# Attention scores by halves of the queries: four quarter tiles of 196 columns, four heads at a time

## The chip, the cores and the metric

The kernel runs on one core of a Trainium2 chip. The metric is the time of one execution on the device in microseconds (us); lower is better. The core has a matrix engine (TensorE: PE for the matmuls, PEld for the weight loads that go with them), a vector engine (DVE), an activation engine (ACT), GpSimd (POOL) and a queue processor (SP) that issues most of the DMAs. Matmuls write to PSUM, which has eight banks of 512 float32 per partition.

## The reference, cut to what matters

```python
scores = scale * np.matmul(q, k.transpose(0, 1, 3, 2))     # batch 2, heads 8, sequence 768, head size 64
is_sink = pos[None, :] < int(n_sink)                       # n_sink 4
in_window = (rel >= 0) & (rel < int(window))               # rel = query - key, window 128
scores = np.where(is_sink | in_window, scores, -1000000000.0)
a = np.exp(scores - np.max(scores, axis=-1, keepdims=True))
a = a / (np.sum(a, axis=-1, keepdims=True) + 1e-09)
x = np.matmul(a, v)
...
x = _moe_ref(x=x, ...)       # 1536 tokens routed to 8 experts of fixed capacity, two layers each
return _moe2_ref(x=x, ...)   # a feed-forward layer with SiLU, 512 to 2048 to 512
```

Each query sees the four sink keys and the 128 keys that end at itself. A block of 128 queries therefore needs its own 128 keys and the 128 of the block before, and of each key place only one of the two: the key of the block before where it lies behind the query's place, the own one otherwise.

## The kernel before

The attention is the first stage. It runs over 12 blocks of 128 queries (2 batches of NB = 6), and in a block over H = 8 heads; a head with its block is a step, n = 0 to 95 (i = n // 8 is the block, j = i % 6 its place in the batch, h = n % 8 the head). The code is one loop over n that writes out the instructions of all engines, and every engine works through its own in the order in which they were written:

- `s_mm` writes the scores by matmuls in float32 (line L261), two heads at a time: it is called at even n. A head has 64 rows of q and k, so two heads lie side by side on the 128 rows of the array (`o` = 0, 1). For j > 0 a matmul makes 264 columns: four sinks and 128 keys of the block before, then the same of the own block. Each head has a bank, a tile of the pool `s`, which holds four tiles and turns in a ring.
- `s_merge` (L267, DVE) overwrites, in the own block's scores, those of the keys that lie behind the query (`later`) by those of the block before. For j = 0 there is nothing to merge.
- `s_max` (L274, DVE) adds the mask, scales and takes the maximum; `s_exp` (L283, ACT) takes the exponential two steps on.
- `tr` (L297, PE) transposes the weights five steps on, and `tr_out` copies them out (ACT) and cuts them into two triangles (POOL); `pv` (L343, L345, L348, PE) multiplies them with the values 13 steps on; `finish` scales on DVE (L370, L366, L377).
- Every eight steps a few more matmuls write to tiles of the pool `s`: `sink_tr` (L326), `vw` (L385, four column quarters of the array with 32 columns each) and `vw_tr` (L396).
- DVE also unpacks weights that come as 64-bit floats (L915 to L931). These instructions are bound to steps: the first one stands at n = 27.
- SP issues the loads (kall, qr, vt, va of a block, then raw weights) in the written order. Eight semaphores serve them in turn, so that a load waits until the one eight before it has landed.

After the attention come the routing (it begins in its last steps), a gather by DMA, the experts and the last feed-forward layer.

Of the kernel before, what the change touches and what calls it, by code (L numbers as in the profile page):

```python
# [11 lines left out]
F32 = mybir.dt.float32  # L12
F32R = mybir.dt.float32r
BF = mybir.dt.bfloat16
I32 = mybir.dt.int32
AF = mybir.ActivationFunctionType
OP = mybir.AluOpType
# [4 lines left out]
P = 128  # L22
B, H, S, D = 2, 8, 768, 64
# [3 lines left out]
KW = P + 4  # L27
# [152 lines left out]


VW = D + E + 1
HH = H // 2
LT, LP, LS = 5, 13, 6
LATE = 9, 10
# [4 lines left out]
PB = {"s": 4, "tp": 2, "X": 2}  # L190
# [3 lines left out]
def attention_band(tc, qd, kd, va_d, vt_d, vs_d, sel_d, wbd_d, eye_d, n_sink, ident, x_d, L_sb, pp, hooks={}):  # L194
    nc = tc.nc
    with ExitStack() as ctx:
        cp = ctx.enter_context(tc.tile_pool(name="a_c", bufs=1))
        wp = ctx.enter_context(tc.tile_pool(name="a_w", bufs=2))

        kall = cp.tile([P, NB, HH, KW], F32, name="kall")  # L200
        va = cp.tile([P, NB, H, VW], F32, name="va")
        vts, Q = {}, {}

        def load(i, step=HH):
            b, j = divmod(i, NB)
# [18 lines left out]
        nc.scalar.dma_start(eye, eye_d)  # L224
        vsf = [cp.tile([97, H, VW], F32, name=f"vsf{b}") for b in range(B)]
        for b in range(B):
# [5 lines left out]
        load(2)  # L232
        vsr = [cp.tile([97, H, VW], F32R, name=f"vsr{b}") for b in range(B)]

        later = cp.tile([P, P], F32, name="later")
        nc.gpsimd.memset(later, 1.0)
        nc.gpsimd.affine_select(out=later, in_=later, pattern=[[1, P]], compare_op=OP.is_gt, fill=0.0, base=0,
                                channel_multiplier=-1)
        mask = cp.tile([P, 3, KW], F32, name="mask")
        nc.gpsimd.memset(mask, 0.0)  # L240
        if n_sink < 4:
            nc.gpsimd.memset(mask[:, :, n_sink:4], NEG)
        nc.gpsimd.affine_select(out=mask[:, 0, 4:], in_=mask[:, 0, 4:], pattern=[[-1, P]], compare_op=OP.is_ge,
                                fill=NEG, base=0, channel_multiplier=1)
        nc.gpsimd.memset(mask[:, 0, 4:4 + n_sink], NEG)
        nc.gpsimd.affine_select(out=mask[:, 1, 4:4 + n_sink], in_=mask[:, 1, 4:4 + n_sink], pattern=[[-1, n_sink]],
                                compare_op=OP.is_ge, fill=NEG, base=0, channel_multiplier=1)

        A, TS, AT, X, XS, LW, VT = {}, {}, {}, {}, {}, {}, {}
        ats = [cp.tile([97, P], F32R, name=f"ats{k}") for k in range(2)]  # L250
        for t in ats:
            nc.gpsimd.tensor_copy(t[96:97, :], later[0:1, 0:1].to_broadcast([1, P]))

        def s_mm(n):
            i, h = divmod(n, H)
            j = i % NB
            b0 = max(j - 1, 0)
            for o in range(2):
                s = pp.tile([P, 512], F32, name="s", bufs=PB["s"])[:, :2 * KW].rearrange("p (a k) -> p a k", a=2)
                d = slice(o * D, (o + 1) * D)  # L260
                nc.tensor.matmul(s[:, :j - b0 + 1], Q[i][d, h // 2], kall[d, b0:j + 1, h // 2], start=True, stop=True)  # L261
                TS[n + o] = s

        def s_merge(n):
            s = TS[n]
            if n // H % NB:
                nc.vector.copy_predicated(s[:, 1, 4:], later.bitcast(I32), s[:, 0, 4:])  # L267

        def s_max(n):
            j = n // H % NB  # L270
            s = TS[n]
            t = wp.tile([P, KW], F32, name="t", bufs=4)
            nm = wp.tile([P, 1], F32, name="nm", bufs=6)
            nc.vector.tensor_tensor_reduce(t, s[:, 1 if j else 0], mask[:, min(j, 2)], -1.0 / math.sqrt(D), 3.0e38,  # L274
                                           OP.add, OP.min, nm)
            TS[n] = t, nm

# [54 lines left out]
        def pv(n):  # L332
# [3 lines left out]
            if r == 0:  # L336
                if (i, g) == (NT - 1, 0):
                    X[i, g] = misc(HH * VW).rearrange("p (h v) -> p h v", h=HH)
                else:
# [82 lines left out]
        NH = NT * H  # L422
        for n in range(NH + LP + 5):
            i, h = divmod(n, H)
            if n < NH and n % 2 == 0:
                s_mm(n)
            if n < len(WARM) - 1:
                warm(WARM[n + 1])
            for f in hooks.get(n, ()):
                if f is None:  # L430
                    while dve_now:
                        feed(dve_now)
                else:
                    f()
            if 0 <= n - 2 < NH:
                s_exp(n - 2)
            if 0 <= n - LT < NH:
                tr(n - LT)
            feed(act_now, act_bg)
            if n < NH and n % 2 == 0:  # L440
                s_merge(n)
                s_merge(n + 1)
            feed(dve_now, dve_bg)
            if n < NH:
                s_max(n)
            feed(dve_now, dve_bg)
            feed(act_now, act_bg)
            for _ in range(3 if n >= NH + LT and n - NH not in LATE else 0):
                feed(act_late)
            it, ht = divmod(n - LS, H)  # L450
            if ht == H - 1 and 0 <= it < NT:
                sink_tr(it)
            if n < NH and h == 0:
                if i == 1:
                    nc.sync.dma_start(vsf[1][:96], vs_d[:96, 1])
                if i + 2 < NT:
                    load_v(i + 2)
                if i + 3 < NT:
                    load(i + 3)
            for at, f in VWS.get(n, ()):  # L460
                (vw, vw_tr, sinks)[f](*at)
            if 0 <= n - LP < NH:
                pv(n - LP)
# [1219 lines left out]
```

## Time and profile before

| | |
|---|---|
| time, median of 3 runs | 556.95 us (555.79 to 557.17) |
| the profiled execution | 556.44 us, its span 554.7 us |
| granted TensorE clock, mean over the span | 0.996 |
| busy over the span | PE 539.3, PEld 478.5, DVE 352.9, ACT 293.6, POOL 227.5 us |

The span goes from the first to the last instruction; what lies around it is 1.7 us here. Matmuls are pipelined and the records overlap, so a busy PE is not one at its peak. The steps of the attention lie between 4 and 97 us, the rest of it and the routing up to 136 us, and the experts and the last layer behind.

### The profile page before, as it was taken

How to read it: one execution, taken by the hardware profiler on the slowest of the kernel's cores; microseconds unless marked ns; L12 is line 12 of the kernel's file. 1: busy time of each engine (PE TensorE's matmuls, PEld its weight loads, DVE VectorE, ACT ScalarE, POOL GpSimd, SP SyncE). 2: the span in 40 equal slices, each digit the busy share in tenths (PEclk: the TensorE clock that was granted, in tenths of full speed). 3: DMA queues.
4: the chain of work that ended last, by engine and by line, in shares of the span. 5: the costliest groups of instructions: out<-in, count | busy, mean ns of one | idle time of the engine just before them, and what ended most of it. 6: DMA issues, size and time to landing. Idle time of an engine off the chain costs nothing.

```text
span 554.7 us, 9683 instructions
## 1 busy us (share of the span) xinstructions
PE 539.3 (97%) x3389; PEld 478.5 (86%) x3389; DVE 352.9 (64%) x983; ACT 293.6 (53%) x576; POOL 227.5 (41%) x218
## 2 busy tenths in 40 slices
PE   8999999878999999999999999999999999999995
PEld 3778777766999999999999989989888988898884
DVE  3788998874433443443337898876979777863523
ACT  4545454675566876776655364453444444443330
POOL 4434234286699999999994000000000000000404
PEclk9999999999999999999999999999999999999999
DMA  7998762244557667667660464653677856266502
GB/s 206 367 389 267 256 205 81 76 142 150 167 199 234 214 222 230 216 221 229 218 223 3 155 219 119 253 186 97 196 253 247 284 162 239 77 210 231 206 19 113
DMA packets 43935, 107.91 MB, mean 195 GB/s; under 512 B 4650, under 2 KB 12458, under 8 KB 43884
## 3 DMA queue, kind: packets, MB, share of 16 engines
q1 hardware_dynamic: 41696, 100.88, 54.0%
q0 software_dynamic: 1920, 6.29, 3.2%
q8 instruction: 27, 0.44, 0.3%
q14 instruction: 24, 0.20, 0.1%
q10 hardware_dynamic: 268, 0.10, 0.1%
HBM read 86.81 MB, written 20.45 MB: 193 GB/s over the span
## 4 chain that ended last, share of the span: by engine, by line
PE 68%; issue 4%; POOL 2%; DMA 1%; ACT 0%; DVE 0%; POOLq 0%; another core or an unknown queue 0%; DVEq 0%; ACTq 0%
PE h L1276 21%; PE acc L1398 20%; PE mm L1182 9%; PE m L1205 8%; PE mm L1185 4%; PE m L1208 4%; POOL out L1369 2%; PE mm L1205 1%; PE mm L1141 1%; DMA row<-x_d,idx 1%; PE mm L1208 1%; PE m L1182 0%; POOLq L1679 0%; PE m L1141 0%; ACT wr L958 0%
## 5 line engine op out<-in xcount | busy, mean ns | idle before, releaser
L961 POOL TENSOR_TENSOR wr<-raw,wr 128x1024 fp32r<-128x1024 f32 x64 | 150.8, 2387 | 8.0 <-ACT wr L958 7.8
L1398 PE MATMUL acc<-wr,gt 128*128 128x512 f32 x576 | 145.4, 395 | 0.0
L1398 PEld LDWEIGHTS acc<-wr,gt 128*128 128x128 f32 x576 | 107.3, 188 | 19.4
L1369 POOL DMA_INDIRECT out<-raw,idx x12 | 11.6, 968 | 241.3 <-DVE raw L1410 241.1
L1276 PE MATMUL h<-x,wr 128*128 128x384 f32 x528 | 101.3, 338 | 0.0
L1276 PEld LDWEIGHTS h<-x,wr 128*128 128x128 f32 x528 | 93.7, 188 | 4.0 <-DVE keep L1310 0.3
L1182 PE MATMUL mm<-xg,wr 128*128 128x384 f32 x248 | 72.4, 360 | 0.5 <-DVE xg L1156 0.3
L958 ACT ACTIVATE wr<-raw 128x1024 fp32r<-128x1024 f32 x64 | 66.6, 1052 | 1.1 <-ACTq L725 0.9
L1205 PE MATMUL m<-ht,wr 128*128 128x384 f32 x224 | 66.0, 361 | 0.0
L1185 PE MATMUL mm<-xg,wr 128*128 128x192 f32 x248 | 62.2, 251 | 0.0
L1208 PE MATMUL m<-ht,wr 128*128 128x192 f32 x224 | 56.2, 251 | 0.0
L1457 DVE TENSOR_TENSOR gt<-keep,gt 128x384 fp32r<-128x384 f32 x64 | 39.1, 613 | 26.7 <-ACT gt L1263 26.6
L283 ACT ACTIVATE A<-t,nm 128x132 f32<-128x132 f32 x96 | 36.1, 400 | 30.3 <-DVE nm L274 30.2
L1182 PEld LDWEIGHTS mm<-xg,wr 128*128 128x128 f32 x248 | 46.5, 187 | 1.2 <-DVE xg L1156 0.7
L1163 DVE TENSOR_TENSOR mm<-mm,t 128x384 f32<-128x384 f32 x33 | 18.7, 567 | 45.2 <-ACT t L1162 41.7
L1185 PEld LDWEIGHTS mm<-xg,wr 128*128 128x128 f32 x248 | 47.3, 191 | 0.0
L1262 ACT ACTIVATE keep<-keep 128x384 f32<-128x384 f32 x30 | 15.8, 526 | 54.0 <-DVE keep L1310 53.9
L1208 PEld LDWEIGHTS m<-ht,wr 128*128 128x128 f32 x224 | 42.7, 191 | 0.0
L1205 PEld LDWEIGHTS m<-ht,wr 128*128 128x128 f32 x224 | 42.0, 188 | 0.0
L305 POOL TENSOR_SCALAR_AFFINE_SELECT atd<-at 128x512 f32<-128x512 f32 x24 | 16.5, 688 | 58.4 <-ACT at L303 47.1
L1276 PE MATMUL h<-xn,wr 128*128 128x384 f32 x180 | 36.8, 339 | 0.0
L1276 PEld LDWEIGHTS h<-xn,wr 128*128 128x128 f32 x180 | 32.6, 188 | 2.6
(197 smaller groups left out, 939.5 us busy)
## 6 DMA issues: line engine op xcount, KB each, us to landing
raw<-in_w SPq DMA_DIRECT2D x64, 512.0 KB, 3.7
sums_d<-os SPq DMA_DIRECT2D x36, 256.0 KB, 2.0
xn<-mix_d SPq DMA_DIRECT2D x12, 768.0 KB, 5.5
raw<-in_wi SPq DMA_DIRECT2D x16, 512.0 KB, 5.7
raw<-in_wo SPq DMA_DIRECT2D x16, 512.0 KB, 6.2
os<-sums_d SPq DMA_DIRECT2D x24, 256.0 KB, 2.6
mix_d<-xn SPq DMA_DIRECT2D x6, 768.0 KB, 4.3
va<-in_va SPq DMA_DIRECT2D x12, 292.0 KB, 4.4
```

The lines of the kernel that those rows point to most:

```text
L283: nc.scalar.activation(A[i][:, h], t, AF.Exp, bias=nm, scale=-1.0)
L958: nc.scalar.activation(w[:, 0, sl], src(), AF.Copy)
L961: (nc.vector if k in self.late else nc.gpsimd).tensor_tensor(w[:, 1, sl], src(), w[:, 0, sl].bitcast(F32), OP.subtract)
L1163: nc.vector.tensor_tensor(h, h, t, OP.add)
L1182: nc.tensor.matmul(mm[:, b, :2 * CAP], w[:, 0, fb, d, o:o + P], x[:, d].rearrange("p a t -> p (a t)"), start=d == 0, stop=False, skip_grou ...
L1185: nc.tensor.matmul(mm[:, b, :CAP], w[:, 1, fb, d, o:o + P], x[:, d, 0], start=False, stop=d == 3, skip_group_check=True)
L1205: nc.tensor.matmul(mm[:, d % 2, :2 * CAP], w[:, 0, d // 2, f, o:o + P], ht[:, f].rearrange("p a t -> p (a t)"), start=c == 0 and f == 0, s ...
L1208: nc.tensor.matmul(mm[:, d % 2, :CAP], w[:, 1, d // 2, f, o:o + P], ht[:, f, 0], start=False, stop=last, skip_group_check=True)
L1276: nc.tensor.matmul(h, w(a, d), x(b, d), start=start and d == 0 and k == 0, stop=d == n - 1 and k == 2, skip_group_check=True)
L1369: i = nc.gpsimd.indirect_dma_start(out=out, out_offset=bass.IndirectOffsetOnAxis(ap=idx[:, t // 3, t % 3:t % 3 + 1], axis=0), in_=o, in_of ...
L1398: nc.tensor.matmul(a, gt[:, u, ts], w[:, v, 2 * p + i], start=(p, i, k) == (0, 0, 0), stop=(p, i, k) == (1, 1, 2), skip_group_check=True)
L1457: later.popleft()()
```

## The change

`s_mm` is called at every fourth n and makes four heads: `r` = 0, 1 are two pairs, and the heads with the same `o` share a bank, 196 columns each. The 128 queries are cut into halves (`a` = 0, 1) that take 64 columns of the array each, so that a pair is made by four quarters of 64 by 64. For j > 0 a quarter gets two matmuls. The first (`outer`, or `t[:, :HB]`) makes the keys of the block before: 128 for the first half of the queries, 64 for the second. The second makes the sinks and the own keys: 68 columns for the first half, 132 for the second. Both halves have 196 columns in all: for the first half the last 64 keys of the block before already lie where `s_max` reads them. `s_merge` has the same 128 elements per query, in two runs of 64 whose source is one run read twice, and `later` is cut accordingly.

```diff
+HB = P // 2
+SW = KW + HB
...
-        later = cp.tile([P, P], F32, name="later")
+        later = cp.tile([P, 2, HB], F32, name="later")
...
+        nc.gpsimd.memset(later[:HB, 1], 0.0)
...
-            b0 = max(j - 1, 0)
-            for o in range(2):
-                s = pp.tile([P, 512], F32, name="s", bufs=PB["s"])[:, :2 * KW].rearrange("p (a k) -> p a k", a=2)
-                d = slice(o * D, (o + 1) * D)
-                nc.tensor.matmul(s[:, :j - b0 + 1], Q[i][d, h // 2], kall[d, b0:j + 1, h // 2], start=True, stop=True)
-                TS[n + o] = s
+            banks = [pp.tile([P, 512], F32, name="s", bufs=PB["s"]) for _ in range(2)]
+
+            def mm(r, o, a, dst, keys, start):
+                d, q = slice(o * D, (o + 1) * D), slice(a * HB, (a + 1) * HB)
+                nc.tensor.matmul(dst(banks[o][q, r * SW:]), Q[i][d, h // 2 + r, q], kall[d, keys[0], h // 2 + r, keys[1]],
+                                 start=start, stop=True, skip_group_check=True)
+
+            def outer(t):
+                return t[:, :2 * KW].rearrange("p (x k) -> p x k", x=2)[:, :, :HB]
+
+            for r in range(2):
+                for o in range(2 if j else 0):
+                    mm(r, o, 0, outer, (j - 1, slice(4, KW)), True)
+                    mm(r, o, 1, lambda t: t[:, :HB], (j - 1, slice(4 + HB, KW)), True)
+                for o in range(2):
+                    k = 4 + HB if j else KW
+                    mm(r, o, 0, lambda t: t[:, HB:HB + k], (j, slice(k)), not j)
+                    mm(r, o, 1, lambda t: t[:, HB:SW], (j, slice(KW)), not j)
+                for o in range(2):
+                    TS[n + 2 * r + o] = banks[o][:, r * SW:(r + 1) * SW]
...
-                nc.vector.copy_predicated(s[:, 1, 4:], later.bitcast(I32), s[:, 0, 4:])
+                nc.vector.copy_predicated(s[:, HB + 4:].rearrange("p (a k) -> p a k", a=2), later.bitcast(I32),
+                                          s[:, :HB].unsqueeze(1).to_broadcast([P, 2, HB]))
...
-            if n < NH and n % 2 == 0:
+            if n < NH and n % 4 == 0:
                 s_mm(n)
```

The order of PE before, from step 21 to step 23 (L326 is `sink_tr`, L385 `vw`, L343 and L345 `pv`, L297 `tr`; a name in brackets is the counter of an engine or of a DMA semaphore that is waited for):

```order
L326 MATMUL s<-ident,a_396 96x128 [waits DVE_49,PE_49,Pool_49]
L385 MATMUL s<-vt,wbd 32x256 [waits DMAHW0_49,DMAHW5_49,DVE_49,PE_49]
L385 MATMUL s<-vt,wbd 32x256 x3
L343 MATMUL X<-va,atd 128x73
L345 MATMUL X<-va,at 128x73
L261 MATMUL s<-kall,qr 128x264 [waits DVE_49,PE_49] x2
L297 MATMUL tp<-ident,A 128x128 [waits Activation_49]
L343 MATMUL X<-va,atd 128x73
L345 MATMUL X<-va,at 128x73
L297 MATMUL tp<-ident,A 128x128 [waits Activation_49]
L343 MATMUL X<-va,atd 128x73
L345 MATMUL X<-va,at 128x73
```

The same steps of PE in the changed kernel, up to the scores of step 24 (lines are 18 higher there: L344 is `sink_tr`, L403 `vw`, L361 and L363 `pv`, L315 `tr`, L264 the scores):

```order
L344 MATMUL s<-ident,a_435 96x128 [waits DVE_49,Pool_49]
L403 MATMUL s<-vt,wbd 32x256 [waits DMAHW5_49,DMAHW0_49,DVE_49]
L403 MATMUL s<-vt,wbd 32x256 x3
L361 MATMUL X<-va,atd 128x73 [waits PE_49]
L363 MATMUL X<-va,at 128x73
L315 MATMUL tp<-ident,A 128x128 [waits Activation_49]
L361 MATMUL X<-va,atd 128x73
L363 MATMUL X<-va,at 128x73
L315 MATMUL tp<-ident,A 128x128 [waits Activation_49]
L361 MATMUL X<-va,atd 128x73
L363 MATMUL X<-va,at 128x73
L264 MATMUL s<-kall,qr 64x2x64 [waits DVE_49]
```

The scores of steps 22 and 23 no longer stand behind `vw` of step 21: they were written with those of step 20. That group of four heads begins on PE like this, and eight rows with the same shapes follow for the second pair:

```order
L361 MATMUL X<-va,atd 128x73
L264 MATMUL s<-kall,qr 64x2x64 [waits DVE_49]
L264 MATMUL s<-kall,qr 64x64
L264 MATMUL s<-kall,qr 64x2x64 [waits Activation_49]
L264 MATMUL s<-kall,qr 64x64
L264 MATMUL s<-kall,qr 64x68
L264 MATMUL s<-kall,qr 64x132
L264 MATMUL s<-kall,qr 64x68
L264 MATMUL s<-kall,qr 64x132
```

Sixteen matmuls in a row have taken the place of two times two.

On DVE, steps 20 to 22 before (L267 is `s_merge`, the two rows of L274 `s_max`, L328 the copy that follows `sink_tr`):

```order
L267 COPY_PREDICATED s<-later,s 128x128 [waits PE_49] x2
L274 ISA t,nm<-s,mask 128x132 [waits DVE_49,Activation_49]
L274 ISA nm 128x1
L370 RECIPROCAL rv<-X 128x4 [waits PE_49]
L274 ISA t,nm<-s,mask 128x132 [waits DVE_49,Activation_49]
L274 ISA nm 128x1
L366 TENSOR_TENSOR lw<-X,rv 128x32 [waits DVE_49]
L267 COPY_PREDICATED s<-later,s 128x128 [waits PE_49] x2
L328 CAST ats_171<-s 96x128
```

The same steps of DVE in the changed kernel (L284 is `s_merge`, L292 `s_max`, L346 the copy):

```order
L284 COPY_PREDICATED s<-later,s 128x128 [waits PE_49]
L284 COPY_PREDICATED s<-later,s 128x128 [waits PE_49,Activation_49]
L292 ISA t,nm<-s,mask 128x132 [waits DVE_49,Activation_49]
L292 ISA nm 128x1
L388 RECIPROCAL rv<-X 128x4 [waits PE_49]
L292 ISA t,nm<-s,mask 128x132 [waits DVE_49,Activation_49]
L292 ISA nm 128x1
L384 TENSOR_TENSOR lw<-X,rv 128x32 [waits DVE_49]
L284 COPY_PREDICATED s<-later,s 128x128
L284 COPY_PREDICATED s<-later,s 128x128 [waits DVE_49]
L346 CAST ats_172<-s 96x128 [waits PE_49]
```

The order is the same. The second pair of merges no longer waits for PE; the first pair waits for the last matmul of its bank, which is one of the second pair's.

## Rows read from the trace of the kernel before

**Rows 1.** Busy time by stage; columns: busy us of each engine, granted clock, DMA share, GB/s.

```profile
9.00:28.00 19.00, 18.32 (x140) 12.33 (x139) 13.38 (x76) 10.81 (x33) 6.87 (x17) 1.00 1.06 358
28.00:60.00 32.00, 32.00 (x254) 24.79 (x254) 26.36 (x139) 16.61 (x46) 12.85 (x27) 1.00 0.93 328
60.00:97.00 37.00, 36.61 (x272) 27.35 (x272) 34.62 (x174) 19.09 (x51) 14.03 (x29) 1.00 0.49 163
97.00:136.00 39.00, 32.19 (x338) 25.98 (x334) 26.67 (x101) 24.89 (x59) 22.15 (x21) 0.96 0.38 125
136.00:555.00 419.00, 412.45 (x2359) 384.72 (x2358) 250.06 (x484) 218.80 (x382) 166.56 (x95) 1.00 0.55 187
```

**Rows 2.** Waits of DVE, 10 to 100 us; columns: us in total, times, longest.

```profile
DVE s L267 <- PE s L261: 9.9, 16, 1.5
DVE t L274 <- PE s L261: 2.2, 2, 1.2
```

**Rows 3.** Timeline of the weight loads around step 47; columns: start, busy us, what.

```profile
46.35 0.30 PEld L343 LDWEIGHTS X<-va,atd 128*128 128x128 f32 x2
46.57 0.30 PEld L345 LDWEIGHTS X<-va,at 128*128 128x128 f32 x2
46.95 0.30 PEld L261 LDWEIGHTS s<-kall,qr 64*128 64x128 f32 x4
47.59 0.14 PEld L297 LDWEIGHTS tp<-ident,A 128*128 128x128 f32 x1 [0.34 <-ACT A L283]
...
48.77 0.30 PEld L261 LDWEIGHTS s<-kall,qr 64*128 64x128 f32 x4
49.19 0.14 PEld L297 LDWEIGHTS tp<-ident,A 128*128 128x128 f32 x1
```

**Rows 4.** Groups by line and shape, 9 to 97 us; busy us, mean ns, idle before.

```profile
L261 PE MATMUL s<-kall,qr 64*128 64x264 f32 x160 | 30.3, 434 | 0.0
...
L267 DVE COPY_PREDICATED s<-later,s 128x128 f32<-128x128 int32 x78 | 19.1, 288 | 10.1 <-PE s L261 9.9
...
L385 PE MATMUL s<-vt,wbd 128*32 128x256 f32 x40 | 3.2, 390 | 0.3 <-issue 0.3
...
L261 PE MATMUL s<-kall,qr 64*128 64x132 f32 x16 | 2.0, 325 | 0.0
```

**Rows 5.** Timeline around steps 21 and 22, then around step 38.

```profile
21.30 0.16 PEld L385 LDWEIGHTS s<-vt,wbd 128*32 128x32 f32 x8 [0.18 <-PE X L348]
21.30 0.64 PE L385 MATMUL s<-vt,wbd 128*32 128x256 f32 x8
...
23.21 0.49 DVE L267 COPY_PREDICATED s<-later,s 128x128 f32<-128x128 int32 x2 [1.50 <-PE s L261]
...
37.77 0.64 PE L385 MATMUL s<-vt,wbd 128*32 128x256 f32 x8
...
38.93 0.75 PE L261 MATMUL s<-kall,qr 64*128 64x264 f32 x4
...
39.68 0.49 DVE L267 COPY_PREDICATED s<-later,s 128x128 f32<-128x128 int32 x2 [1.38 <-PE s L261]
```

**Rows 6.** SP's waits, 20 to 29 us, then timeline of SP and DVE.

```profile
SPq L893 <- DMA vt<-in_vt: 1.1, 1, 1.1
...
SPq L209 <- DMA raw<-in_wi: 0.3, 1, 0.3
...
20.88 1.75 SPq L893 DMA_DIRECT2D raw<-in_wi  x3
...
27.58 0.33 SPq L209 DMA_DIRECT2D qr<-in_qd  x1
...
28.19 0.42 DVE L915 TENSOR_SCALAR f<-raw 128x512 int32<-128x512 int32 x1
```

**Rows 7.** Timeline of POOL and DVE at the start.

```profile
3.80 0.20 POOL L236 MEMSET later<- 128x128 f32 x1
...
5.31 0.30 DVE L274 CUSTOM_DVE_ANT_0 t<-s,mask 128x132 f32<-128x132 f32 x1 [4.12 <-POOL mask L245]
...
7.98 0.30 DVE L274 CUSTOM_DVE_ANT_0 t<-s,mask 128x132 f32<-128x132 f32 x1 [0.98 <-PE s L261]
```

More of the change, by code (lines that the diff above doesn't have):

```diff
@@ L233, in attention_band @@
         vsr = [cp.tile([97, H, VW], F32R, name=f"vsr{b}") for b in range(B)]
-        later = cp.tile([P, P], F32, name="later")
+        later = cp.tile([P, 2, HB], F32, name="later")
         nc.gpsimd.memset(later, 1.0)
-        nc.gpsimd.affine_select(out=later, in_=later, pattern=[[1, P]], compare_op=OP.is_gt, fill=0.0, base=0,
+        nc.gpsimd.affine_select(out=later, in_=later, pattern=[[HB, 2], [1, HB]], compare_op=OP.is_gt, fill=0.0, base=0,
                                 channel_multiplier=-1)
+        nc.gpsimd.memset(later[:HB, 1], 0.0)
         mask = cp.tile([P, 3, KW], F32, name="mask")
@@ L251, in attention_band @@
         for t in ats:
-            nc.gpsimd.tensor_copy(t[96:97, :], later[0:1, 0:1].to_broadcast([1, P]))
+            nc.gpsimd.tensor_copy(t[96:97, :], later[0:1, 0, 1:2].to_broadcast([1, P]))
         def s_mm(n):
@@ L273, in s_max @@
             nm = wp.tile([P, 1], F32, name="nm", bufs=6)
-            nc.vector.tensor_tensor_reduce(t, s[:, 1 if j else 0], mask[:, min(j, 2)], -1.0 / math.sqrt(D), 3.0e38,
+            nc.vector.tensor_tensor_reduce(t, s[:, HB:], mask[:, min(j, 2)], -1.0 / math.sqrt(D), 3.0e38,
                                            OP.add, OP.min, nm)
```

## The prediction, made before the changed kernel ran

> **What bounds the kernel now.** I read the busy times by stage first [rows 1]. The steps of the attention lie in the first three stages. PE is covered by records nearly throughout (18.32 of 19, 32.00 of 32, 36.61 of 37 us), which alone says little, since matmul records overlap. DVE is idle for 19.00 - 13.38 = 5.6 us, then 32.00 - 26.36 = 5.6 us, then only 37.00 - 34.62 = 2.4 us. So I read what DVE waits for [rows 2]: 9.9 us before a merge and 2.2 us before a maximum, all of it for the score matmuls of L261. DVE holds no other large wait. Up to 60 us PE sets the pace and DVE waits for scores; from 60 us on DVE is 94% busy and sets it itself. The third limit is the DMA: its share is 1.06 between 9 and 28 us and 0.93 up to 60 us [rows 1], and SP's own waits there are for landings [rows 6]. Behind 97 us nothing that the change touches runs, so whatever the attention gains there arrives at the end, and a stage of 419 us follows unchanged.
>
> **What the change takes off PE.** The timeline of weight loads prices a pair of heads. The load of L261 comes at 46.95 and the next operation's at 47.59, 0.64 us later [rows 3]. Ahead of it, two loads follow two others after 0.22 us (46.35, 46.57), so the regular place was 46.79; the load came at 46.95, and going over to the half array costs 0.16. A pair is 0.80 us, four heads are 1.60. For j = 0, with 132 columns, it is 49.19 - 48.77 = 0.42, with 0.16 ahead 0.58. The difference, 0.22 us for 132 columns fewer in two passes (160 records for 80 heads [rows 4]), is 0.83 ns a column and pass; the means of the two shapes say the same, (434 - 325) / 132 [rows 4]. So 0.44 of the 0.64 us is columns, and 0.20 is fixed: the first weights and the way out.
>
> A group of four heads after: each quarter makes 196 columns twice per pair, 2 x 196 x 0.83 = 0.325 us, two pairs 0.65. With 0.16 ahead and 0.20 fixed it is 1.01 us instead of 1.60, 0.59 less. For j = 0 it is 2 x 0.22 + 0.36 = 0.80 instead of 1.16, 0.36 less. Of the fixed part I take nothing off for weights of half as many columns. The loads between the matmuls must hide: regular loads of 128 columns are 0.11 us apart [rows 3], those of 64 should take half, 0.055, and the shortest matmul streams 64 x 0.83 = 0.053. That just hides.
>
> This rests on four quarters running at once, which no row shows. The nearest row is L385: four column quarters of the array, all on the same 128 rows, with 256 columns and two passes. Its eight matmuls take 0.64 us together, its eight loads 0.16 [rows 5]; one after another the columns alone would take 8 x 256 x 0.83 = 1.7 us. So column parts overlap fully, and in L261 the two row parts do (0.64 us for four matmuls of 264 columns, which make 0.88 one after another). I take four at once. The bounds are four and one.
>
> By stage: steps 8 to 27 hold 5 groups, 5 x 0.59 = 3.0 us; steps 28 to 59 hold 6 and 2 with j = 0, 3.5 + 0.7 = 4.3 us; steps 60 to 95 hold 9, 5.3 us. PE gets 12.6 us.
>
> **What of it arrives.** Up to 28 us: nearly nothing. Two landings stand in the way that compute can't hasten, since SP's loads wait for each other's landing. `vw` at step 21 needs the vt of blocks 2 and 3, the later of which lands at about 20.9 us (SP's wait for it ends before its row at 20.88 [rows 6]); `vw` started at 21.30 [rows 5], 0.4 us later. And the first unpack instruction stands at step 27, and nothing behind it in DVE's queue can pass it: its raw weights land just before 27.58 (SP's row there had waited for it), and it ran at 28.19 [rows 6]. If DVE comes to it earlier it stands, and behind it the maxima of all later heads. So this stage gives at most 28.19 - 27.58 = 0.6 us, not 3.0.
>
> From 28 to 60 us PE saves 4.3, DVE has 5.6 idle. The order helps too: scores of a later step no longer stand behind `vw`, which was what DVE's longest waits were (1.50 us at 23.21, 1.38 us at 39.68, each with L385 between [rows 5]). Against it, the first merge now waits for four heads' matmuls. Before, it started 39.68 - 38.93 = 0.75 us after the first load [rows 5]; that becomes 0.75 - 0.44 + 0.65 = 0.96, once in a group of four. Up to 8 x 0.2 = 1.6 us, where PE is what DVE waits for; I take 0.6. Net 3.7.
>
> From 60 to 97 us DVE's idle time caps it at 2.4; a queue that is worked in order won't lose its last waits, and I take 1.2.
>
> **The rest of the change** I cost at nothing. The merge has the same 128 elements, 0.29 us [rows 4]; were its broken pattern a tenth dearer, the 80 merges would cost DVE 2.3 us, about half of it in stages where DVE sets the pace, and this stays in the range. The added memset on POOL is at most the 0.20 us of the one of twice the width and rows [rows 7]; it delays the mask, for which the first maximum waits at 5.31, but DVE later waits 0.98 us for the scores of step 4 [rows 7], which are the next group and no earlier than before. Without that cover it costs its 0.20. A group asks for two tiles of the ring of four instead of four, so scores wait for the reads of heads at least five steps back, no tighter than before; behind a waiting group PE holds `tr` and `pv`, and ACT and DVE wait for those.
>
> Sum: 0.6 + 3.7 + 1.2 = 5.5 us off. The profiled execution took 556.44 us, half a microsecond below the median of the runs (556.95) and within their range. I forecast 551.0 us.
>
> **The rivals.** First, the other sign: the quarters don't run at once. The place is the group itself. If the two column halves of the same rows go one after another, loads included, a pair takes 2 x (128 + 64 + 68 + 132) x 0.83 = 0.65 us of columns and eight loads of 0.055, 1.09 in all, and a group 0.36 + 2.18 = 2.54 instead of 1.60, 0.94 more. The 11 full groups up to 60 us pay that in full, since PE sets the pace there: 10.3 us; of the nine behind, 8.5 us, DVE's pace hides a part that no row gives. 567 to 575 us. It decides at two streams at once, where a group is 0.36 + 4 x 0.325 = 1.66, as long as before. The rows of L385 speak against it: its loads of one part do overlap with the streams of another on the same rows [rows 5].
>
> The Trainium skill, TensorE: Matmul & The Clock Gate, section Part 3: Packing small matmuls (The mechanism), speaks for that rival: it says that weight loads overlap with matmuls in flight only where the row group differs, and two of the four quarters share theirs. By that rule the time would be this rival's, 567 to 575 us; by the rows of L385 it is the forecast.
>
> Second, no change to be measured (0.3%, 1.7 us, is about what a run here can tell from none): the waits move instead of going. DVE's idle time from 28 to 60 us would have to turn into waits at the head of each group and for `pv` (the reciprocals follow PE within a step or two), and DVE's own work would hold the rest. For it speaks that DVE has 26.4 us of work in those 32 already; against it that its waits name the score matmuls and nothing else [rows 2]. That leaves the 0.6 and some tenths: 555 to 556.5 us.
>
> Third, more: the raw weights land earlier, or DVE's waits go entirely. Then the first stage gives its 3.0, the second 4.3, the third 2.4: 9.7 us, 546.7. Against it speaks the DMA share of 1.06 [rows 1].
>
> **How the numbers follow.** Forecast 0.66; third rival 0.12; second 0.14; first 0.08. Faster than 555.3 are the forecast and the third: 0.78. Within 0.3%: 0.14. Slower: 0.08. The range leaves out the first rival and the far end of the third: 547.5 to 556.3.
>
> **What would show it.** Right: from the first load of a score group to the next operation's load 0.85 us in the changed kernel, 0.64 for j = 0; `vw` of step 21 at 20.9 to 21.1 us and the first unpack at 27.6, both at their landing; DVE's idle time from there to 60 us of 1 to 2 us; the steps over at about 91.5 us; the long stage behind still some 419 us. Wrong: a group of 1.5 us or more (the first rival); DVE waits for the scores that stay at ten (the second); an unpack that starts well before 27 us (the third).

## The result, and the profile after

The changed kernel takes 551.32 us (median of 4 runs, 550.22 to 552.11), the kernel before 557.06 (4 runs, 555.79 to 557.71): a ratio of 0.9888, interval 0.9869 to 0.9907. It is 5.7 us faster; 551.0 was forecast, with a range of 547.5 to 556.3. The profiled execution took 551.16 us with a span of 549.4 (before 556.44 and 554.7), so its span is 5.3 us shorter. Three of the twelve runs of experiment 8 had a mean granted clock of 0.865 to 0.917 and took 591.5 to 619.8 us; its figures go without them. Lines after: L264 for the scores, L284 for the merge, and from the maximum on 18 higher than before, L292 for the maximum, L403 for `vw`, L933 for the first unpack.

The busy times by stage of the changed kernel; columns as in [rows 1]. The last row begins 5 us earlier than the one of before, as the long stage does now.

```profile
9.00:28.00 19.00, 16.97 (x298) 13.89 (x296) 13.13 (x78) 11.14 (x36) 6.77 (x17) 1.00 1.06 356
28.00:60.00 32.00, 30.93 (x436) 27.27 (x435) 29.98 (x151) 18.10 (x49) 14.03 (x28) 1.00 1.00 354
60.00:97.00 37.00, 33.82 (x478) 29.84 (x479) 35.90 (x181) 21.18 (x56) 17.54 (x35) 1.00 0.47 157
97.00:136.00 39.00, 32.34 (x316) 25.34 (x316) 22.80 (x82) 22.38 (x53) 23.37 (x16) 0.91 0.40 131
131.00:549.00 418.00, 412.22 (x2358) 384.71 (x2358) 249.96 (x484) 218.62 (x382) 166.18 (x95) 1.00 0.55 188
```

DVE's idle time is the third busy time taken from the length of the stretch: 5.9 us up to 28 us (5.6 before), 2.0 up to 60 (5.6 before), 1.1 up to 97 (2.4 before). Two things stand out. The first stage kept its idle time. And from 97 to 136 us the granted clock is 0.91, where it was 0.96.

DVE's waits from 10 to 100 us in the changed kernel (us in total, times, longest), to be read beside [rows 2]:

```profile
DVE s L284 <- PE s L264: 5.2, 5, 1.6
DVE f L933 <- DMA raw<-in_wi: 1.0, 1, 1.0
DVE t L292 <- PE s L264: 1.0, 1, 1.0
```

Waits for scores fell from 12.1 us in 18 places to 6.2 in 6. A wait of 1.0 us for the raw weights has come in.

The weight loads of score groups in the changed kernel (start, busy us, what, and in brackets the idle time ahead with its releaser), to be read beside [rows 3]. The group at 23.25 is that of step 24, the one at 48.71 has j = 0.

```profile
23.25 0.76 PEld L264 LDWEIGHTS s<-kall,qr 64*64 64x64 f32 x32
...
48.71 0.43 PEld L264 LDWEIGHTS s<-kall,qr 64*64 64x64 f32 x16
49.32 0.14 PEld L315 LDWEIGHTS tp<-ident,A 128*128 128x128 f32 x1 [0.18 <-issue]
...
59.17 0.19 PEld L264 LDWEIGHTS s<-kall,qr 64*64 64x64 f32 x4
60.96 0.74 PEld L264 LDWEIGHTS s<-kall,qr 64*64 64x64 f32 x28 [1.59 <-DVE ats L346]
...
63.28 0.76 PEld L264 LDWEIGHTS s<-kall,qr 64*64 64x64 f32 x32
64.12 0.14 PEld L315 LDWEIGHTS tp<-ident,A 128*128 128x128 f32 x1
```

Thirty-two loads of four heads are through in 64.12 - 63.28 = 0.84 us, where two pairs took 2 x 0.64; for j = 0 it is 0.61. The group at 59.17 shows something new: it stands inside for 1.59 us, because its second bank is freed only by DVE's copy behind `sink_tr` (L346).

Shapes of the changed kernel, 9 to 97 us (busy us, mean ns, idle before), to be read beside [rows 4]:

```profile
L284 DVE COPY_PREDICATED s<-later,s 128x128 f32<-128x128 int32 x80 | 19.4, 285 | 5.5 <-PE s L264 5.2 <-PE s L414 0.2
...
L264 PEld LDWEIGHTS s<-kall,qr 64*64 64x64 f32 x672 | 17.3, 133 | 6.3 <-DVE ats L346 4.2 <-issue 0.6
```

A merge takes 285 ns, as before (288). The stops for L346 cost the weight loads 4.2 us in all.

The places that answer to [rows 5 to 7] and the last maximum of the steps, in the changed kernel (DVE, SP and PEld in order of time):

```profile
5.99 0.29 DVE L292 CUSTOM_DVE_ANT_0 t<-s,mask 128x132 f32<-128x132 f32 x1 [4.79 <-PE s L264]
...
10.46 0.29 DVE L292 CUSTOM_DVE_ANT_0 t<-s,mask 128x132 f32<-128x132 f32 x1
...
20.95 1.80 SPq L911 DMA_DIRECT2D raw<-in_wi  x3
...
21.04 0.19 PEld L403 LDWEIGHTS s<-vt,wbd 128*32 128x32 f32 x8 [0.51 <-DVE nm L292]
...
24.26 0.49 DVE L284 COPY_PREDICATED s<-later,s 128x128 f32<-128x128 int32 x2 [1.60 <-PE s L264]
...
27.75 0.43 DVE L933 TENSOR_SCALAR f<-raw 128x512 int32<-128x512 int32 x1 [1.02 <-DMA raw<-in_wi]
...
57.03 0.28 DVE L292 CUSTOM_DVE_ANT_0 t<-s,mask 128x132 f32<-128x132 f32 x1
...
92.98 0.28 DVE L292 CUSTOM_DVE_ANT_0 t<-s,mask 128x132 f32<-128x132 f32 x1
```

and the maxima of the same two steps (59 and 95) in the kernel before:

```profile
61.05 0.28 DVE L274 CUSTOM_DVE_ANT_0 t<-s,mask 128x132 f32<-128x132 f32 x1
...
99.34 0.29 DVE L274 CUSTOM_DVE_ANT_0 t<-s,mask 128x132 f32<-128x132 f32 x1
```

`vw` of step 21 starts at 21.04, just behind the landing that let SP go on at 20.95; the profile says that a read by DVE (L292) released it, which ends at the same place, so this one profile can't tell the two apart. The unpack starts at 27.75 (28.19 before), and waited for its data: 0.4 us gained. Step 59 is 61.05 - 57.03 = 4.0 us ahead, step 95 is 99.34 - 92.98 = 6.4 us ahead. The end is only 554.7 - 549.4 = 5.3 ahead: about 1 us is given back behind the steps.

### The profile page after: what moved, and what is told of

Same layout as the page of the kernel before. It is cut to its first block, busy times and chain, and to the rows that moved or that the text cites. A ratio compares the mean times of both kernels' runs of the same rounds, so it can differ in the third digit from the quotient of the medians.

```text
span 549.4 us, 10689 instructions
## 1 busy us (share of the span) xinstructions
PE 529.3 (96%) x3901; PEld 480.2 (87%) x3901; DVE 352.0 (64%) x983; ACT 293.2 (53%) x576; POOL 228.5 (42%) x219
## 4 chain that ended last, share of the span: by engine, by line
PE 69%; issue 4%; POOL 2%; DMA 1%; ACT 0%; DVE 0%; POOLq 0%; another core or an unknown queue 0%; DVEq 0%; ACTq 0%
PE h L1294 21%; PE acc L1416 21%; PE mm L1200 9%; PE m L1223 8%; PE mm L1203 4%; PE m L1226 4%; POOL out L1387 2%; PE mm L1223 1%; PE mm L1159 1%; DMA row<-x_d,idx 1%; PE mm L1226 1%; PE m L1200 0%; POOLq L1697 0%; PE m L1159 0%; ACT wr L976 0%
## 5 line engine op out<-in xcount | busy, mean ns | idle before, releaser
L1181 DVE TENSOR_TENSOR mm<-mm,t 128x384 f32<-128x384 f32 x33 | 18.7, 566 | 45.2 <-ACT t L1180 45.2
```

The costliest lines, as they stand in the source:

```text
L1181: nc.vector.tensor_tensor(h, h, t, OP.add)
```

## The experiments

They were run in three groups, each beside the kernel before on the same chip: its medians there were 558.05 us (first four), 557.28 (next four) and 557.72 (last three).

**1. The same quarters, two heads at a time.**

```diff
-            for r in range(2):
+            for r in range(1):
...
-            if n < NH and n % 4 == 0:
+            if n < NH and n % 2 == 0:
```

> The quarters alone: 196 columns in four quarter tiles as in the change, but two heads at a time, each with its own bank, at every even step as before. Theory (what counts is the time that PE is occupied, as far as DVE and the landings leave room): a pair should take about 0.52 us from its first load to the next operation's instead of 0.64, and two pairs with 0.16 ahead 1.36 us instead of 1.60, so PE gets 0.24 us per four heads, 1.4 us from 28 to 60 us and at most 1.2 behind: about 554.5 us. Rival (the gain comes from the order, scores that no longer stand behind vw): nothing of it is here, 556 to 557 us. Second rival (the gain is the shorter matmuls, four at a time adds nothing): 551 to 552 us.

Measured: 553.68 us (552.82 to 554.83), ratio 0.9928, interval 0.9908 to 0.9947. That is 0.8 below the 554.5 expected, and neither rival's time. A pair takes 0.50 us of weight loads instead of 0.64 (0.52 was expected):

```profile
33.34 0.42 PEld L264 LDWEIGHTS s<-kall,qr 64*64 64x64 f32 x16
33.84 0.14 PEld L315 LDWEIGHTS tp<-ident,A 128*128 128x128 f32 x1
```

The quarters alone bring 4.4 us. Two pairs of 0.50 with their two ways into the half array cost more than one group of 0.84 with one; its last maximum starts at 95.38 us, 4.0 ahead of the kernel before, where the whole change is 6.4 ahead. How much of the rest is PE's shorter time, and how much the order (scores that no longer stand behind `vw`), no run tells apart.

**2. Each group's matmuls issued twice.**

```diff
-            for r in range(2):
+            for r in (0, 1, 0, 1):
```

> The changed kernel with every group's score matmuls issued twice, so that four heads again occupy PE for about 1.65 us (0.16 ahead, 1.50 to the next load; before it was 1.60), while the grouping by four and the order stay. Theory of PE's occupied time: the gain goes nearly all, 555.5 to 557.5 us. Rival of the order: the gain stays nearly all, 551 to 553 us. Between them each has its share.

Measured: 561.59 us (561.20 to 563.90), ratio 1.0074, interval 1.0052 to 1.0095: slower than before, beyond the expectation. The group and DVE's largest wait:

```profile
60.20 1.43 PEld L264 LDWEIGHTS s<-kall,qr 64*64 64x64 f32 x64
61.73 0.14 PEld L315 LDWEIGHTS tp<-ident,A 128*128 128x128 f32 x1
```

```profile
DVE s L284 <- PE s L264: 15.5, 15, 2.6
```

A group takes 61.73 - 60.20 = 1.53 us, with 0.16 ahead 1.69, against 1.60 for four heads before; over 24 groups that is 2.2 us. The last maximum starts at 104.63, 5.3 later than before. So some 3 us go to the group's being one piece: the first merge waits for all of it, and DVE's wait before merges (from 9 to 97 us) is 15.5 us, where it was 9.9; and the weight loads stand 2.6 us inside groups for DVE's copy (L346), as in the changed kernel. Four heads in one group pay only because the group is short. How the 5.3 us divide is worked out, not measured.

**3. The unpack two steps later.**

```diff
-FIRST, EVEN, ODD = 18, (...), (*range(27, 49, 2), *range(53, 93, 2))
+FIRST, EVEN, ODD = 18, (...), (*range(29, 51, 2), *range(53, 93, 2))
```

> The changed kernel with the first unpack instruction at step 29 instead of 27 and the others of that series one place on (one falls to step 49), so that DVE comes to it after its raw weights have landed. Theory (the landing capped the first stage; DVE stood 1.0 us for it): about 0.8 us less than the changed kernel, 550.5 us, and no wait of DVE for raw. Rival (the scores of step 28 or the landing for vw would have held DVE anyway): 551.3 us, unchanged.

Measured: 551.44 us (548.69 to 553.51), ratio 0.9877, interval 0.9850 to 0.9903. No difference from the change that the runs can tell, and they are wide apart: at a mean clock of 0.997 and 1.0 two runs took 548.69 and 549.87, at 0.983 two took 553.25 and 553.51. Inconclusive by itself; the last experiment comes back to it.

**4. The copy behind `sink_tr` on ACT instead of DVE.**

```diff
-            if i < NT - 1:
-                dve_now.appendleft(lambda: nc.vector.tensor_copy(ats[i % 2][:96], tp))
-            else:
-                act_now.appendleft(lambda: nc.scalar.activation(ats[i % 2][:96], tp, AF.Copy))
+            act_now.appendleft(lambda: nc.scalar.activation(ats[i % 2][:96], tp, AF.Copy))
```

> The changed kernel with the copy that follows sink_tr on ACT instead of DVE in all blocks. Theory (from 28 us on DVE sets the pace): DVE is rid of eleven copies of 0.28 us, 3.1 us, some 2.5 of them where it is the pace setter: 548.5 to 549.5 us. Rival (ACT, or PE's wait for the copy, which becomes no shorter if ACT comes to it later, holds the pace): 551 to 552 us.

Measured: 550.31 us (549.18 to 555.21), ratio 0.9895, interval 0.9856 to 0.9933. That lies between the 548.5 to 549.5 expected and the rival's 551 to 552: by the medians undecided. The trace is clearer. The weight loads' stop inside groups falls from 4.2 to 0.5 us, and the last maximum starts at 90.68, 2.3 us earlier than in the changed kernel:

```profile
L264 PEld LDWEIGHTS s<-kall,qr 64*64 64x64 f32 x672 | 16.4, 133 | 2.4 <-ACT ats L345 0.5 <-issue 0.3
```

```profile
55.86 0.28 DVE L292 CUSTOM_DVE_ANT_0 t<-s,mask 128x132 f32<-128x132 f32 x1
...
90.68 0.28 DVE L292 CUSTOM_DVE_ANT_0 t<-s,mask 128x132 f32<-128x132 f32 x1
```

Eleven copies of 0.277 us taken off DVE are 3.0 us. From step 59 to step 95 this kernel takes 90.68 - 55.86 = 34.82 us, the changed one 92.98 - 57.03 = 35.95: 1.1 less, which is about four copies. DVE sets the pace there. But the span, 548.0, is only 1.4 us shorter: 0.9 of the 2.3 is lost again behind the steps.

**5 and 6. Both kernels without the merges.**

```diff
-            if n // H % NB:
+            if False:
```

> The kernel before without its 80 merges: the scores of the keys of the block before are left out of the own block's scores, all else runs. It takes 80 x 0.29 = 23 us off DVE. Theory (until 60 us PE sets the pace, and behind it PE is covered as well, 36.6 of 37 us): little comes of it, 0.5 to 2.5 us off the kernel before, and the steps' last maximum starts at 97 to 99 us instead of 99.3. Rival (DVE's own work sets the pace before the change too): 8 us or more off.

> The changed kernel without its 80 merges, which leaves the same part out. Theory (after the change DVE sets the pace, so that what PE saved beyond 6.4 us lies hidden behind DVE's work): now PE sets it again, and most of its 12.6 us arrive, less the 2.5 us that the landings of the first stage keep: 8 to 10 us below the kernel before without merges, where the two kernels with merges are 5.7 apart. Rival (what holds the rest back is the ring of the score tiles and the first wait of a group, not DVE's work): still 5 to 6.5 us apart.

Measured: 571.13 us (570.60 to 572.09) and 562.23 (561.24 to 565.68), 8.9 apart. Both are slower than the kernels with merges, where experiment 5 was expected below the kernel before. All of that lies behind the steps: from the last maximum to the end they take 471.3 and 471.1 us, where the kernels with merges take 455 to 458, and 20.4 us of it are at the lower clock in both. Other scores send other data through the routing; that this is the reason is likely, not shown. So they are compared with each other, and by their steps. DVE's largest wait and the maxima of steps 59 and 95, first of the kernel before without merges, then of the changed one:

```profile
DVE t L274 <- PE s L261: 18.7, 27, 1.5
```

```profile
60.86 0.28 DVE L274 CUSTOM_DVE_ANT_0 t<-s,mask 128x132 f32<-128x132 f32 x1
...
97.55 0.28 DVE L274 CUSTOM_DVE_ANT_0 t<-s,mask 128x132 f32<-128x132 f32 x1
```

```profile
DVE t L292 <- PE s L264: 13.5, 13, 4.2
```

```profile
56.70 0.28 DVE L292 CUSTOM_DVE_ANT_0 t<-s,mask 128x132 f32<-128x132 f32 x1
...
89.21 0.28 DVE L292 CUSTOM_DVE_ANT_0 t<-s,mask 128x132 f32<-128x132 f32 x1
```

Before the change 23 us less work on DVE bring the steps 1.8 us, and turn into 18.7 us of waiting for scores: PE set the pace, from step 59 on too (36.69 us up to step 95 instead of 99.34 - 61.05 = 38.29, for 36 merges of 0.29 less). After it they bring 92.98 - 89.21 = 3.8 us. The changed kernel without merges is 8.3 us ahead of its counterpart at the last maximum (with merges 6.4), and 8.9 at the end, as the theory had it.

**7. PE kept busy at 100 us.**

```diff
+            if n == NH + LP - 1:
+                m = misc(512)
+                for _ in range(7):
+                    nc.tensor.matmul(m, zero[:, :P], zero, start=True, stop=True)
```

> The changed kernel with seven more matmuls of 512 columns on zeros behind the last value matmul, where PE stood idle for 1.6 us at 100 us (they add no term to any result). Theory (the 1.15 us given back in the routing is the granted clock of 0.5 for 6.8 us instead of 3.4, after PE had been idle): the low stretch shrinks to 3.4 us or goes, the mean clock is 0.997 or more, 549.0 to 550.3 us. Rival (it was given back by waits of the routing, whatever the clock): 551.0 to 552.0, with the clock better or not.

Measured: 550.06 us (549.66 to 550.52), ratio 0.9865, interval 0.9846 to 0.9884: as the theory said, at the upper end. The interval overlaps that of the change (0.9869 to 0.9907), so by the times alone the gain isn't shown; and the mean clock, expected at 0.997 or more, was 0.992 to 0.994 in three of the four runs. In the profiled one it fell at 18 and 62 us instead, before the place that was filled. PE in the changed kernel, then with the matmuls on zeros (six of the seven have a record):

```profile
99.75 0.38 PE L366 MATMUL X<-vsr,ats 97*128 97x292 f32 x1
101.75 0.43 PE L688 MATMUL s<-oh,G 128*128 128x8 bf16 x11 [1.63 <-DVE G L675]
```

```profile
100.50 0.38 PE L366 MATMUL X<-vsr,ats 97*128 97x292 f32 x1
100.95 1.46 PE L485 MATMUL s<-zero 128*128 128x512 bf16 x6
102.50 0.42 PE L692 MATMUL s<-oh,G 128*128 128x8 bf16 x11
```

Windows of the kernel before, of the changed one, and of experiment 9, which has the same matmuls on zeros (columns as above; the clock is the third figure from the right):

```profile
106.10:108.70 2.60, 0.82 (x14) 0.63 (x14) 2.40 (x10) 1.69 (x6) 0.00 (x0) 1.00 0.08 31
110.10:113.40 3.30, 3.19 (x26) 2.31 (x25) 2.19 (x7) 2.61 (x6) 0.30 (x1) 0.50 0.22 79
```

```profile
99.80:101.10 1.30, 0.33 (x3) 0.11 (x2) 1.20 (x4) 0.81 (x3) 0.00 (x0) 1.00 0.04 14
101.20:107.90 6.70, 5.89 (x48) 4.43 (x49) 4.39 (x16) 4.67 (x13) 1.65 (x2) 0.50 0.11 42
```

```profile
100.00:108.00 8.00, 6.86 (x72) 5.12 (x70) 6.64 (x25) 5.22 (x15) 2.89 (x3) 1.00 0.10 35
```

PE idles in both kernels while the routing waits for DVE, and then works at 0.50 of full speed (1.2 instead of 2.4 GHz): for 3.4 us before, for 6.8 after. With the idle time filled the clock stays at 1.00 there.

**8. Neighbours in the queue on the same rows.** In the changed kernel the four quarters take turns: the two column halves of one row half, then the two of the other. Neighbours in the queue always lie in different columns, but only every second pair of them in different rows, which the expectation below puts too strongly. Here all matmuls of one row half stand ahead of those of the other.

```diff
-            for r in range(2):
-                for o in range(2 if j else 0):
-                    mm(r, o, 0, outer, (j - 1, slice(4, KW)), True)
...
+            for o in range(2):
+                for r in range(2):
+                    if j:
+                        mm(r, o, 0, outer, (j - 1, slice(4, KW)), True)
...
```

> The changed kernel with the group's matmuls in another order: all of the heads in rows 0 to 63 first, then all in rows 64 to 127, so that neighbours in the queue differ only in their columns of the array. Theory (four quarters run at once because neighbours lie in different rows and columns; matmuls start in the order of the queue): two at once, the group takes 0.85 + 0.65 = 1.5 us on PE, as many as the kernel before needs for four heads, but the first bank is complete at half of that; 555 to 559 us. Rival 1 (quarters of the same rows go one after another): 2.5 us a group, 567 us or more. Rival 2 (the queue reaches far enough for the order not to matter): 0.85 us a group and 550.5 to 552 us.

Measured: nine runs took 552.49 to 556.25 us, their middle one 554.28; ratio 0.9951, interval 0.9934 to 0.9968. A group:

```profile
65.39 1.15 PEld L264 LDWEIGHTS s<-kall,qr 64*64 64x64 f32 x32
66.62 0.14 PEld L315 LDWEIGHTS tp<-ident,A 128*128 128x128 f32 x1
```

It takes 66.62 - 65.39 = 1.23 us (another one 1.37): not 2.5 (one after another), not 0.84 (order without effect). Two column halves of the same rows do run at once, and the order of the queue decides how far the other rows join in. The size was off: 1.5 was expected, and the time came out 0.7 us below the expected range. Why it is less than 1.5 isn't shown.

**9 to 11. Both cures together, the later unpack on top, and the changed kernel once more.** Experiment 9 has the edits of 4 and 7, experiment 10 that of 3 as well, experiment 11 none.

> The changed kernel with both edits: the copy behind the sinks' transpose on ACT, and the seven matmuls on zeros that fill PE's idle time at 100 us. Theory (each cures a loss of its own, DVE's pace from 60 us on and the granted clock in the routing): the last maximum starts at 90.5 to 91.5 us as with the copy alone, and from there to the end of the span it takes 454.5 to 455.5 us, as in the kernels with no low clock behind 95 us, instead of 457.3; 546.5 to 548.5 us. Rival (PE, idle more in the steps, falls to the low clock elsewhere and loses there what it won): 549.5 to 551.

> The same with the first unpack two steps later (step 29), so that DVE no longer stands 0.8 us at 27 us for the raw weights. Theory (the landing is what holds the first stage's gain back at that place, and DVE's pace takes over behind it): 0.3 to 0.8 us less than the last kernel, 546 to 548 us. Rival (DVE reaches the next scores no earlier, as PE is late by the wait of the value matmul at 21 us): within 0.3 us of the last kernel.

> The changed kernel once more, as it was predicted, beside the two others on the same chip and with more runs: 550.2 to 552.1 us as before, the runs at a mean clock of 0.997 about 1 us below those at 0.993.

Measured: 548.49 us (5 runs, 547.69 to 548.52), ratio 0.9831, interval 0.9815 to 0.9848; 549.68 (546.84 to 551.92), ratio 0.9865, interval 0.9841 to 0.9888; 551.89 (549.64 to 553.13), ratio 0.9892, interval 0.9870 to 0.9915. Experiment 9 is the best kernel of the study by its median, 9.2 us below the one before, at the upper end of what was expected; its last maximum, at 91.83, is 0.3 later than expected, its stretch behind (below) as expected. Experiment 11 came out higher than expected in three of its six runs (above 552.1), and its runs don't follow their mean clock: 551.03 at 0.985, 552.90 at 0.992. Experiment 10 reaches lower, 546.84 and 547.78 at a mean clock of 0.998, but its other four runs have 0.984 to 0.992 and take 549.4 to 551.9, so the later unpack isn't shown to gain at the end, and even with the idle time filled the mean clock isn't up in every run. In its trace the unpack starts without a wait:

```profile
26.31 0.29 DVE L292 CUSTOM_DVE_ANT_0 t<-s,mask 128x132 f32<-128x132 f32 x1
27.96 0.29 DVE L292 CUSTOM_DVE_ANT_0 t<-s,mask 128x132 f32<-128x132 f32 x1
28.17 0.42 DVE L934 TENSOR_SCALAR f<-raw 128x512 int32<-128x512 int32 x1
```

Step 27 is 1.4 us ahead of experiment 4's (26.31 against 27.69), step 28 only 0.4 (27.96 against 28.34); of experiment 9's, step 28 is 1.4 ahead (29.36).

How far single profiles of the same steps agree: the start of the maximum of step 28, and the time from there to step 59 and to step 95.

| kernel | step 28 | 28 to 59 | 59 to 95 |
|---|---|---|---|
| before | 29.50 | 31.55 | 38.29 |
| changed; 11; 7 | 28.74; 30.03; 29.36 | 28.29; 28.36; 28.38 | 35.95; 35.94; 35.98 |
| 3 | 29.95 | 27.66 | 35.97 |
| 4; 9; 10 | 28.34; 29.36; 27.96 | 27.52; 27.64; 27.51 | 34.82; 34.83; 34.83 |

From step 28 on equal steps repeat within 0.2 us; ahead of it they scatter by more than 1. Experiments 4 and 9 have the same code up to step 95 and the clock at 1.00 there, and yet their step 28 is 1.02 us apart: the raw weights let the unpack start at 27.35 in one and at 28.37 in the other, 1.02 apart as well. From step 59 on experiments 7 and 3 hold a test that nobody planned. For some 3.4 us, from 62.6 and from 61.7, PE had only half the clock, and the steps took as long as ever. Steps 59 to 95 of the kernel before, of the changed one and of experiment 7, then the slow part of the last (columns as in [rows 1]):

```profile
61.05:99.34 38.29, 37.90 (x284) 28.53 (x285) 35.84 (x179) 18.99 (x51) 14.55 (x29) 1.00 0.46 156
```

```profile
57.03:92.98 35.95, 32.99 (x489) 28.82 (x482) 35.66 (x180) 19.05 (x52) 15.46 (x29) 1.00 0.55 184
```

```profile
57.74:93.72 35.98, 33.89 (x489) 30.12 (x481) 35.70 (x179) 19.06 (x51) 15.58 (x29) 0.95 0.57 192
62.65:66.00 3.35, 3.35 (x34) 3.22 (x36) 3.35 (x19) 1.75 (x5) 1.86 (x5) 0.50 0.83 273
```

What the stretch behind the steps costs, by kernel: from the start of the last maximum to the end of the span, and how long PE had the lower clock within it (without the last 5 us or so of the span, where every kernel has it).

| kernel | last maximum | end of span | between | at 0.5 |
|---|---|---|---|---|
| 7, 8, 9, 10 | 93.72, 95.91, 91.83, 90.30 | 548.8, 550.7, 546.7, 545.0 | 455.1, 454.8, 454.9, 454.7 | 0 |
| before | 99.34 | 554.7 | 455.4 | 3.4 |
| changed; 11; 1; 2; 4 | 92.98; 94.33; 95.38; 104.63; 90.68 | 549.4; 551.0; 552.0; 560.4; 548.0 | 456.4; 456.7; 456.6; 455.8; 457.3 | 6.8 |
| 3 | 93.58 | 551.8 | 458.2 | 10.2 |

But for the matmuls on zeros and one copy the stretch is the same work in all rows. Its length rises with the time at the lower clock, though not by that alone: with 6.8 us it lies anywhere from 455.8 to 457.3. All three kernels that fill the idle time (7, 9, 10) have no lower clock there; of the eight others in the table, only 8 has none, though PE idles 1.63 us there too. The profiles of 3, 7 and 11 have a mean clock of 0.91 from 9 to 28 us as well, and their steps end later than those of the changed kernel's first profile.

## Why the prediction was right, point by point

**The group on PE: right.** 0.85 us from the first load to the next operation's was forecast, 0.84 measured; 0.64 for j = 0, and 0.61. With the 0.16 ahead it saves 2 x 0.80 - 1.00 = 0.60 (forecast 0.59). By the prediction's sum 0.65 of it is what the columns take with four streams at once. Experiment 8 shows that this needs an order in which the quarters take turns.

**The first rival: ruled out.** Quarters of the same rows are not worked one after another: the group would take 2.5 us, and even in the order made for it (experiment 8) it takes 1.23. The rule of the Trainium skill, TensorE: Matmul & The Clock Gate, section Part 3: Packing small matmuls (The mechanism), that weight loads overlap with matmuls in flight only where the row group differs, would, taken alone, have given 567 to 575 us. The trace disagrees with it here: the group takes 0.84 us where 2.5 would go with it, and the changed kernel took 551.3.

**Up to 28 us: the mechanism right, the size not to be told.** The landings hold the stage, as forecast: `vw` at 21.04, the unpack at 27.75 after 1.02 us of waiting for its data, 0.4 us earlier than before where 0.6 was forecast. But the landing alone shifts by 1.0 us between two profiles (experiments 4 and 9), and step 28 with it, so 0.4 can't be told from 0.6, nor from nothing. How much is hidden behind that wait is as unsure: with it gone (experiment 10) step 28 gains 0.4 or 1.4, by the profile that it is compared with. DVE's idle time here, 5.9 us, now lies mostly before merges, 1.60 of it at 24.26 for the group behind `vw`.

**28 to 60 us: right.** 4.0 - 0.4 = 3.6 us arrived; 3.7 was forecast. From step 28 to step 59, which three profiles repeat, it is 31.55 - 28.29 = 3.3. DVE's idle time fell to 2.0, the upper end of the 1 to 2 forecast. The first merge of step 24 starts 24.26 - 23.25 = 1.01 us after the first load, where 0.96 was worked out. That a long group has a price is shown by experiment 2; the 0.6 us given to it in the sum was not measured by itself.

**60 to 97 us: mis-sized.** "A queue that is worked in order won't lose its last waits, and I take 1.2": 38.29 - 35.95 = 2.3 us arrived, nearly all of DVE's idle time, which between these two maxima fell from 38.29 - 35.84 = 2.45 us to 35.95 - 35.66 = 0.29. DVE waits for no scores from 60 us until the steps are over. From there it sets the pace alone: experiment 4 took four copies off it and gained four copies, without merges (experiment 6) the steps from 59 to 95 took 35.95 - 32.51 = 3.4 us less, and half the clock on PE for 3.4 us cost them nothing (experiments 3 and 7). The steps are over 6.4 us earlier than at 97, at 90.6 (91.5 was forecast). So what PE saved there beyond 2.3 of its 5.3 us lies behind DVE's work, as the term's cap had it. That DVE set the pace there before the change too, as the prediction read it, isn't so: experiment 5 took some 10 us off DVE in these steps and gained 1.6. PE set it, with DVE little behind; the cap is the same.

**Behind 97 us: no term for the clock.** The prediction took it that whatever the attention gains arrives at the end. In this pair of profiles about 1 of 6.4 us did not; the long stage from 131 us on still takes 418. The lower clock lasts 6.8 us instead of 3.4 and falls on the routing's matmuls, and filling PE's idle time before it (experiment 7) shortened the stretch by 456.4 - 455.1 = 1.3 us. So the clock is the likely cause. It isn't shown to be the whole one: stretches with the same 6.8 us differ by 1.5, and in experiment 8 PE idled as long and the clock stayed up.

Nor do these runs show it as a cost of the change, since the clock differs from run to run in both kernels. Of the 39 runs of the kernel before beside the experiments, seven had a mean clock of 0.997 (555.92 to 557.46 us, the middle one 556.23) and twelve 0.993 (557.93 to 558.86, the middle 558.3). Of the ten of the changed kernel two had 0.997 (549.64 and 550.22) and three 0.993 (551.16 to 552.11). At equal mean clock the kernels are 6.3 and 6.8 us apart, about the 6.4 of the steps: then the gain does arrive at the end, as far as so few runs tell. Why PE's idle time is followed by 3.4 us of lower clock in one run, 6.8 in another and none in a third stays open.

So in this pair of profiles two errors cancelled, and that the forecast came so close is in part luck: 0.4 + 3.6 + 2.3 - 1.0 = 5.3 us by the spans, where 0.6 + 3.7 + 1.2 = 5.5 was forecast.

**The rest: not all at nothing.** The merge cost what it cost before. The memset delays nothing: the first maximum starts at 5.99 us instead of 5.31 [rows 7], but it now waits for the scores of the whole first group, not for the mask. At step 8 (10.46, before 10.42) no loss is to be seen, though other profiles with the same code up to there have 10.04 (experiment 7) to 11.20 (experiment 11), so that some tenths couldn't be. The ring was called "no tighter than before", and that was wrong: a group of two tiles needs them at one time, and the second is one that `sink_tr` filled and only DVE empties; PE's weight loads stand 4.2 us for it. It cost the changed kernel little, as DVE was late itself; experiment 4 removed both the stop and the copy, so its 2.3 us don't tell what the stop alone is worth. They also hold the landing's scatter: from step 28 to step 95 experiments 4 and 9 gain 1.9 and 1.8 on the changed kernel.

**The second and third rival.** The waits did not merely move (12.1 us for scores became 6.2). The third had the waits gone entirely, and came half true: from 60 us on, but not in the first stage, for the reason given.

## What to carry to other kernels

A shorter piece of work on a waited-for engine is worth at most the idle time of the engine that waits, stage by stage, and that much can arrive in full; beyond it the other engine's own work is the price of everything. Small matmuls can share the array by rows and columns at once, but their order in the queue decides how many run together, and a group should be short, since the first reader waits for all of it. When a gain upstream vanishes downstream, compare the granted clock of the same work before looking for waits, and runs of equal clock before calling the gain lost; here a few matmuls on zeros in PE's idle time shortened the stretch behind the steps by 1.3 us in the traces. And before reading tenths from a pair of profiles, see how far two profiles of the same code differ at that place.

## What the runs showed of the hardware

- Four quarters of 64 by 64 in float32 take 0.84 us for 32 loads and matmuls if the four take turns in the queue, and 1.23 (another group 1.37) if all of one row half stand ahead of the other's. One after another the prediction's sum makes 2.5.
- Where PE isn't waited for, half its clock cost nothing: 3.4 us at 0.50 in experiment 7, and steps 59 to 95 took 35.98 us, with the full clock 35.95.
- The runs of experiment 8 line up by their mean granted clock: 552.5 and 552.6 us at 0.997, 554.2 to 554.3 at 0.993, and 555.9 to 556.3 at 0.989. Those of experiment 11 do not.
